# Three of the last output blocks: the residual stored first, the gated sums added onto it by DMAs with addition

## The chip, the cores and the metric

The kernel runs on one core of a Trainium2 chip. The metric is the device time of one execution in microseconds. A core has a matrix engine (PE, with its weight loads PEld), a vector engine (DVE), a scalar engine (ACT), a general one (POOL), and SP, which here only issues DMAs. ACT and POOL can issue DMAs too. All DMAs are carried out by the same 16 DMA engines. PE writes its sums to PSUM, which DVE and ACT read; POOL works on SBUF alone.

## The reference

One input x of 2048 tokens by 512 channels is normalized. Attention with 32 heads of 16 channels is computed from it, and beside it a token-mixing MLP, whose silu is the gate:

```python
x = A_x
xn = _layernorm(x, axis=-1)
s = _A_ref(xn, A_wqkv, A_wo)                            # softmax attention, times wo
g = _silu(_B_ref(xn, B_w1, B_b1, B_w2, B_b2))           # mixer over tokens: w1, gelu, w2
return x + s * g
```

Everything is float32. Matrix products in which precision counts are made of three products of upper and lower halves.

## The kernel before

The 2048 tokens are 16 blocks of 128 rows (`NB = 16`, `P = 128`, `D = 512`), so a block of the output is a tile of 128 x 512 float32, 256 KB. The kernel computes the projections, then runs one long loop in which PE alternates between the scores of attention, their row maxima, the values (`values`, whose accumulator is the bank `av`) and pieces of the mixer's and the output projection's products, which fill the gaps. The order is written out by hand; each engine executes its own instructions in that order and waits on semaphores for the others. SP's queue is in order as well.

For the output projection the four groups of heads are multiplied with wo. Of the blocks 8 to 15, three groups are summed early, the gate g of each block is loaded into a tile `gates[b]`, and `ys[b]` holds the residual x plus s times g over those three groups. The `ys` of the blocks 8 to 11 are quarters of one tile named `big`, those of 12 to 15 quarters of another. The tiles of `gates[b]` are called `wh`, `wl` or `raw` in the profile: 8 `wh`, 9 `wl`, 10 `wh`, 11 `wl`, 12 `wh`, and 13, 14 and 15 `raw`.

The last group of heads is complete only after the last step of attention. The code at the end of the kernel then does for each block 8 to 15: three matmuls (`Last.times`, L1389) of that group into a PSUM bank (`mx` or `sc`); the gate, a product of the bank with `gates[b]`, on DVE (`gate`, L1398) or, for block 10, by way of ACT and POOL (`gate_aside`, L1394 and L1395); and `send` (L1402 and L1403), an addition of `ys[b]` on POOL or DVE and a store of the result from SP's or ACT's queue. POOL adds for the blocks 8 to 12, DVE for 13 to 15. For the blocks 10 to 15 a piece of attention's own division is in between (`ways`, with the two subtractions on L107).

Of the kernel before, what the change touches and what calls it, by code (L numbers as in the profile page):

```python
# [11 lines left out]
OP = mybir.AluOpType  # L12
# [9 lines left out]
def tile_attention_token_mixer(ctx, tc, x, wqkv, wo, w1, b1, w2, b2, out):  # L22
    nc = tc.nc
    P = 128
# [78 lines left out]
    def av_bank():  # L103
        return ps_av.tile([P, 512], F32, name="av")
# [594 lines left out]
    def silu(j, ps):  # L699
        y = el.tile([P, D], F32, name="ev")  # L700
        t = el.tile([P, D], F32, name="t", bufs=4)
        nc.scalar.activation(y, ps, AF.Identity, bias=b2h[:, j : j + 1], scale=0.25)
        after(2, lambda: nc.scalar.activation(t, y, AF.Tanh))

        def gate():
            nc.gpsimd.tensor_scalar(t, t, 1.0, None, op0=OP.add)
            nc.gpsimd.tensor_tensor(out=t, in0=t, in1=y, op=OP.mult)
            after(2, lambda: nc.sync.dma_start(g_d[j], t))

        after(4, gate)  # L710
# [4 lines left out]
    def put_away(p, span, half, av):  # L715

        if (p, half) == (NP - 1, 1):
            return
        ev = el.tile([P, 512], F32, name="ev")
        copied(ev, av)  # L720
        if p == NP - 1:
            own(span, half, ev)
            return
        g, i = divmod(p, 4)
        if i == 0:
            dens[span] = sm.tile([P, 64], F32, name="d")
        rows = ev.rearrange("(j r) q -> r j q", r=32)
        for a in range(2):
            h = 2 * i + a
            nc.sync.dma_start(  # L730
                dens[span][DH * h : DH * (h + 1), :],
                rows[16 - 16 * a, 2 * a : 2 * a + 2, :].rearrange("c (j q) -> c j q", q=64),
            )
        nc.sync.dma_start(num_d[g][span][160 * i : 160 * i + P, :], ev)
        if i == 3 or p == NP - 2:
            invert(g, span)
# [165 lines left out]
    ys = {}  # L902
# [68 lines left out]
    gates = {}  # L971
# [11 lines left out]
    def step(t):  # L983

        p, r = divmod(t, SPP)
        span, i = divmod(r, NB)
        at = span * 1024
        if (p, span) != (NP - 1, QH - 1):
            return p, span, None, (i, i), (at, at + 512), i == 0, i == NB - 1
        half, i = divmod(i, NB // 2)  # L990
        at += 512 * half
        return p, span, half, (2 * i, 2 * i + 1), (at, at), i == 0, i == NB // 2 - 1
# [14 lines left out]
    def values(t):  # L1007
        p, span, half, kbs, qat, first, last = step(t)
        if first:
            state["av"] = av_bank()  # L1010
        av = state["av"]
        for a in range(2):
            for c in range(2):
                j = 2 * a + c
                nc.tensor.matmul(  # L1015
                    av[32 * j : 32 * j + 32, :],
                    vps[p][:, kbs[c], 16 * a : 16 * a + 32], prob.pop((t, a, c)),
                    start=first, stop=last,
                )
        if last:  # L1020
            soon.append(lambda: put_away(p, span, half, av))
# [357 lines left out]
    class Last:  # L1379
# [15 lines left out]
            nc.gpsimd.tensor_tensor(out=gates[self.b], in0=t, in1=gates[self.b], op=OP.mult)  # L1395

        def gate(self):
            nc.vector.tensor_tensor(out=gates[self.b], in0=self.ps, in1=gates[self.b], op=OP.mult)  # L1398

        def send(self, eng, queue=nc.sync):  # L1400
            b = self.b
# [1 line left out]
            queue.dma_start(out[b * P : (b + 1) * P, :], gates[b])  # L1403

    lasts = {}
    for b in (8, 9):
        lasts[b] = Last(b).times(3)
        lasts[b].gate()
    for v in (NT - 2, NT - 1):
        values(v)  # L1410
    for b in (8, 9):
        lasts[b].send(nc.gpsimd)
    while later or soon:
# [21 lines left out]
    ways[1].back(1, *parts_[1])  # L1435
    ways[1].upper(1, *parts_[1])
    lasts[11].gate()
    lasts[11].send(nc.gpsimd)
    ways[1].lower(1, *parts_[1])
    for b in range(12, NB):  # L1440
        lasts[b] = Last(b).times(3)
    for b in range(12, NB):
        lasts[b].gate()
    lasts[12].send(nc.gpsimd)
    lasts[13].send(nc.vector, nc.scalar)
    lasts[14].send(nc.vector)
    lasts[15].send(nc.vector, nc.scalar)

# [26 lines left out]
```

## Time and profile before

| | us |
|---|---|
| median of 3 runs | 1634.22 (1633.86 to 1634.64) |
| the profiled execution | 1634.06 |
| its span | 1632.2 |
| PE busy | 1621.9 (99%) |
| DVE busy | 1418.1 (87%) |
| ACT busy | 1194.5 (73%) |
| POOL busy | 575.4 (35%) |

The span is the time from the first to the last instruction that the profiler saw. The granted clock of PE was 0.998 of full speed over the span. In a row of the timeline the first number is the start in us, the second the duration of the group, followed by the engine, the source line, the operation, the tile that is written and those that are read, the shape, and the count. In a table by windows each engine's busy time stands in us with the number of instructions, then PE's clock, the DMA engines' busy share and their rate. In an account of one line, the numbers after a group are the least, median and largest duration of one instruction in ns, then the first and last start in us.

### The profile page before, as it was taken

Reading aid. Unit: us, or ns where it says so; the run is one execution under the profiler, and the core shown is the slowest. Engines: PE = TensorE matmul, PEld = TensorE weight load, DVE = VectorE, ACT = ScalarE, POOL = GpSimd, SP = SyncE. Lnnn points to the kernel's source line nnn. Section 1 sums busy time; section 2 is a strip of 40 time slices with the busy share of each in tenths; the row PEclk is TensorE's granted clock in tenths of the full one; section 3 lists DMA queues with packets and bytes.
Section 4 is the critical chain, followed back from the end, with each engine's and each line's share of the span. In section 5 each row is a group of like instructions: output and inputs, shape, how many; then the busy total and the mean of one; then the engine's idle time right before and its main releaser. Section 6 shows DMA issues by size and latency. Waiting matters only on the chain.

```text
span 1632.2 us, 31813 instructions
## 1 busy us (share of the span) xinstructions
PE 1621.9 (99%) x11948; PEld 892.0 (55%) x11948; DVE 1418.1 (87%) x2506; ACT 1194.5 (73%) x2297; POOL 575.4 (35%) x676
## 2 busy tenths in 40 slices
PE   9999999999999999999999999999999999999998
PEld 7888845555554545555555545555554545544554
DVE  7655989999999999999999999999999999999955
ACT  4333488777877777787777777787777777788785
POOL 0223743333443334332433223223222332662434
PEclk9999999999999999999999999999999999999999
DMA  6479621415133141836150522305152515354344
GB/s 226 174 247 227 122 59 47 82 34 95 41 53 76 38 79 35 191 121 111 37 85 18 99 57 46 70 30 77 37 85 59 91 37 78 100 110 134 117 151 168
DMA packets 150775, 152.89 MB, mean 94 GB/s; under 512 B 51340, under 2 KB 109708, under 8 KB 147548
## 3 DMA queue, kind: packets, MB, share of 16 engines
q1 hardware_dynamic: 146044, 149.70, 38.8%
q8 instruction: 94, 1.54, 0.4%
q0 software_dynamic: 4288, 0.62, 0.3%
q14 instruction: 61, 0.50, 0.1%
q10 hardware_dynamic: 288, 0.52, 0.1%
HBM read 99.63 MB, written 50.32 MB: 92 GB/s over the span
## 4 chain that ended last, share of the span: by engine, by line
PE 98%; DVE 1%; ACT 0%; DMA 0%; SPq 0%; issue 0%; DVEq 0%; ACTq 0%
PE av L1015 31%; PE sc L1165 16%; PE sc L1000 10%; PE sc L537 8%; PE mx L1000 8%; PE mx L1165 7%; PE mx L537 6%; PE sc L440 3%; PE mx L440 2%; PE mx L1112 1%; PE sc L1112 1%; PE sc L1215 1%; PE av L440 1%; PE sc L116 1%; PE sc L114 1%; PE sc L115 1%
## 5 line engine op out<-in xcount | busy, mean ns | idle before, releaser
L541 DVE TENSOR_REDUCE mxp<-sc 128x1 f32<-128x512 f32 x1129 | 735.9, 681 | 74.7 <-PE sc L537 49.7
L1005 ACT ACTIVATE prob<-sc 128x512 f32<-128x512 f32 x1135 | 638.3, 604 | 168.8 <-PE sc L1000 98.2
L541 DVE TENSOR_REDUCE mxp<-mx 128x1 f32<-128x512 f32 x919 | 606.0, 681 | 50.3 <-PE mx L537 30.9
L1005 ACT ACTIVATE prob<-mx 128x512 f32<-128x512 f32 x913 | 523.1, 606 | 127.3 <-PE mx L1000 71.7
L1015 PE MATMUL av<-prob,vp 128*32 128x512 f32 x4096 | 543.0, 604 | 0.0
L537 PE MATMUL sc<-big 48*128 48x512 f32 x1129 | 427.8, 417 | 0.0
L1000 PE MATMUL sc<-big 50*128 50x512 f32 x1135 | 423.1, 417 | 0.2 <-ACT prob L1005 0.2
L1165 PE MATMUL sc<-hu,wh 64*128 64x512 f32 x1072 | 359.3, 404 | 0.0
L537 PE MATMUL mx<-big 48*128 48x512 f32 x919 | 349.9, 416 | 0.1
L1000 PE MATMUL mx<-big 50*128 50x512 f32 x913 | 346.9, 415 | 0.5 <-ACT prob L1005 0.5
L1000 PEld LDWEIGHTS sc<-big 50*128 50x128 f32 x1135 | 198.2, 185 | 137.9 <-DVE mxp L541 102.0
L537 PEld LDWEIGHTS sc<-big 48*128 48x128 f32 x1129 | 196.9, 185 | 81.7 <-ACT prob L1005 53.5
L1165 PEld LDWEIGHTS sc<-hu,wh 64*128 64x128 f32 x1072 | 193.9, 184 | 58.8 <-issue 41.9
L1000 PEld LDWEIGHTS mx<-big 50*128 50x128 f32 x913 | 162.2, 185 | 107.4 <-DVE mxp L541 83.3
L1165 PE MATMUL sc<-hu,wl 64*128 64x512 f32 x536 | 215.1, 401 | 0.0
L537 PEld LDWEIGHTS mx<-big 48*128 48x128 f32 x919 | 160.9, 185 | 74.4 <-ACT prob L1005 38.1
L1015 PEld LDWEIGHTS av<-prob,vp 128*32 128x32 f32 x4096 | 81.8, 108 | 171.8 <-issue 161.4
L1165 PE MATMUL mx<-hu,wh 64*128 64x512 f32 x464 | 156.2, 405 | 0.0
L179 POOL CAST wh<-raw 128x512 fp32r<-128x512 f32 (+1 forms) x105 | 61.3, 584 | 255.2 <-PE sc L537 57.7
L107 POOL TENSOR_TENSOR wl<-raw,wh 128x512 fp32r<-128x512 f32 (+1 forms) x113 | 136.6, 1210 | 28.9 <-ACT wh L181 20.4
L562 POOL CAST m<-f 16x128 fp32r<-16x128 f32 x32 | 9.0, 280 | 311.2 <-DVE f L552 308.4
L1165 PEld LDWEIGHTS sc<-hu,wl 64*128 64x128 f32 x536 | 98.8, 184 | 13.3 <-issue 5.9
(240 smaller groups left out, 1592.0 us busy)
## 6 DMA issues: line engine op xcount, KB each, us to landing
raw<-in_B_w_dram SPq DMA_DIRECT2D x93, 256.0 KB
big<-k_d SPq DMA_DIRECT2D x96, 128.0 KB
big<-q_d SPq DMA_DIRECT2D x96, 128.0 KB
q_d<-sg SPq DMA_DIRECT2D x16, 512.0 KB
k_d<-sg SPq DMA_DIRECT2D x16, 512.0 KB
num_d<-ev SPq DMA_DIRECT2D x30, 256.0 KB
u_d<-uo SPq DMA_DIRECT2D x14, 512.0 KB
hu<-u_d SPq DMA_DIRECT2D x14, 512.0 KB
```

The costliest lines, as they stand in the source:

```text
L107: eng.tensor_tensor(out=o, in0=a, in1=b.bitcast(F32), op=OP.subtract)
L114: nc.tensor.matmul(ps, wh, mh, start=first, stop=False)
L115: nc.tensor.matmul(ps, wh, ml, start=False, stop=False)
L179: nc.gpsimd.tensor_copy(whs[n][:, :m, :], raws[n][:, :m, :])
L440: nc.tensor.matmul(ps, w[part][:, kd, m], xt[kd][:, z, :], start=w is wh and z == 0 and kd == 0, stop=w is wl and kd == ND - 1,)
L537: nc.tensor.matmul(ps, q[o : o + 48, r * P : (r + 1) * P], k[o : o + 48, c * 512 : (c + 1) * 512], start=True, stop=True,)
L541: return nc.vector.tensor_reduce(mxp[u // 16][:, a, r % 8, c : c + 1], ps, axis=AX.X, op=OP.max)
L1000: nc.tensor.matmul(ps, ks[p][o : o + 50, kb * P : (kb + 1) * P], qs[p][o : o + 50, at : at + 512], start=True, stop=True,)
L1005: return nc.scalar.activation(e, ps, AF.Exp, scale=scale)
L1015: nc.tensor.matmul(av[32 * j : 32 * j + 32, :], vps[p][:, kbs[c], 16 * a : 16 * a + 32], prob.pop((t, a, c)), start=first, stop=last,)
L1112: nc.tensor.matmul(ps(a), w(r), m(r), start=first, stop=last)
L1165: i = nc.tensor.matmul(ps(), w(r), m(r), start=first and first_half, stop=last and not first_half)
```

## The change

For the blocks 11, 12 and 13 the addition of the residual leaves POOL and DVE. Before the last blocks are finished, SP stores `ys[b]`, which then holds all but the last group's part, to the output. The gate of these blocks writes its product into `ys[b]` itself, in place of `gates[b]`. At the end POOL issues three DMAs that add `ys[b]` onto the rows already in the output. The blocks 14 and 15 are added on DVE and stored as before.

```diff
         def gate(self):
-            nc.vector.tensor_tensor(out=gates[self.b], in0=self.ps, in1=gates[self.b], op=OP.mult)
+            to = ys[self.b] if self.b in onto else gates[self.b]
+            nc.vector.tensor_tensor(out=to, in0=self.ps, in1=gates[self.b], op=OP.mult)
...
     lasts = {}
+    onto = ()
     for b in (8, 9):
         lasts[b] = Last(b).times(3)
         lasts[b].gate()
     for v in (NT - 2, NT - 1):
         values(v)
+    onto = (11, 12, 13)
+    for b in onto:
+        nc.sync.dma_start(out[b * P : (b + 1) * P, :], ys[b])
     for b in (8, 9):
         lasts[b].send(nc.gpsimd)
...
     lasts[11].gate()
-    lasts[11].send(nc.gpsimd)
     ways[1].lower(1, *parts_[1])
     for b in range(12, NB):
         lasts[b] = Last(b).times(3)
     for b in range(12, NB):
         lasts[b].gate()
-    lasts[12].send(nc.gpsimd)
-    lasts[13].send(nc.vector, nc.scalar)
+    for b in onto:
+        nc.gpsimd.dma_start(out[b * P : (b + 1) * P, :], ys[b], accum_op=OP.add)
     lasts[14].send(nc.vector)
     lasts[15].send(nc.vector, nc.scalar)
```

On SP, at the end of the program, the queue changes as follows; names in brackets are the semaphores waited for (DMAHW and DMASW those of DMAs issued by SP or ACT and by POOL, the others those of engines):

```order
-L1403 DMA out_dram<-wh 128x512 [waits DMAHW7_49,Pool_49]
-L1403 DMA out_dram<-wl 128x512 [waits DMAHW0_49,Pool_49]
-L1403 DMA out_dram<-wh 128x512 [waits DMAHW1_49,Pool_49]
-L1403 DMA out_dram<-wl 128x512 [waits DMAHW2_49,Pool_49]
-L1403 DMA out_dram<-wh 128x512 [waits DMAHW3_49,Pool_49]
-L1403 DMA out_dram<-raw 128x512 [waits DMAHW5_49,DVE_49]
+L1415 DMA out_dram<-big 128x512 [waits DMAHW7_49]
+L1415 DMA out_dram<-big 128x512 [waits DMAHW0_49]
+L1415 DMA out_dram<-big 128x512 [waits DMAHW1_49]
+L1404 DMA out_dram<-wh 128x512 [waits DMAHW2_49,Pool_49]
+L1404 DMA out_dram<-wl 128x512 [waits DMAHW3_49,Pool_49]
+L1404 DMA out_dram<-wh 128x512 [waits DMAHW4_49,Pool_49]
```

Three stores from `big` stand ahead of the stores of the blocks 8, 9 and 10; the stores of 11 and 12 are gone, and that of 14 follows unchanged.

On POOL, the end of the program, from the additions of the blocks 8 and 9 on:

```order
-L1402 TENSOR_TENSOR wh<-big,wh 128x512 [waits DVE_49]
-L1402 TENSOR_TENSOR wl<-big,wl 128x512 [waits DVE_49]
+L1403 TENSOR_TENSOR wh<-big,wh 128x512 [waits DVE_49]
+L1403 TENSOR_TENSOR wl<-big,wl 128x512 [waits DVE_49]
 L1395 TENSOR_TENSOR wh<-t,wh 128x512 [waits DMAHW4_49,Activation_49]
-L1402 TENSOR_TENSOR wh<-big,wh 128x512 [waits Pool_49]
-L1402 TENSOR_TENSOR wl<-big,wl 128x512 [waits DVE_49]
-L1402 TENSOR_TENSOR wh<-big,wh 128x512 [waits DVE_49]
+L1403 TENSOR_TENSOR wh<-big,wh 128x512 [waits Pool_49]
+L1449 DMA out_dram<-big 128x512 [waits DMAHW7_49,DVE_49]
+L1449 DMA out_dram<-big 128x512 [waits DMAHW0_49,DVE_49]
+L1449 DMA out_dram<-big 128x512 [waits DMAHW1_49,DVE_49]
```

The additions of the blocks 11 and 12 have given way to three DMAs, each of which waits for its residual's store (DMAHW7, 0 and 1) and its gate on DVE.

On DVE, the gates of the blocks 11 to 15 and the additions behind them:

```order
-L1398 TENSOR_TENSOR wl<-sc,wl 128x512 [waits DMAHW3_49,PE_49]
+L1399 TENSOR_TENSOR big<-sc,wl 128x512 [waits DMASW5_49,DMASW4_49,DMASW6_49,DMASW3_49,DMASW7_49,DMASW2_49,DMAHW3_49,DMASW1_49,DMAHW7_49,DMASW0_49,PE_49]
 L107 TENSOR_TENSOR hu<-mx,hu 32x256 [waits Activation_49]
-L1398 TENSOR_TENSOR wh<-mx,wh 128x512 [waits DMAHW2_49,PE_49]
-L1398 TENSOR_TENSOR raw<-mx,raw 128x512 [waits PE_49]
-L1398 TENSOR_TENSOR raw<-sc,raw 128x512 [waits PE_49] x2
-L1402 TENSOR_TENSOR raw<-big,raw 128x512 [waits DVE_49] x3
+L1399 TENSOR_TENSOR big<-mx,wh 128x512 [waits DMAHW2_49,DMAHW0_49,PE_49]
+L1399 TENSOR_TENSOR big<-mx,raw 128x512 [waits DMAHW1_49,PE_49]
+L1399 TENSOR_TENSOR raw<-sc,raw 128x512 [waits PE_49] x2
+L1403 TENSOR_TENSOR raw<-big,raw 128x512 [waits DVE_49] x2
```

One of three additions is gone from DVE, and the gates of 11, 12 and 13 wait for the stores of the residual whose tiles they overwrite. ACT's queue keeps one store of two, that of block 15.

## The prediction

> **What bounds the kernel now.** I read the page first, then the last 17 us of the timeline engine by engine, then the table by windows of the same stretch, then the accounts of single source lines.
>
> ```profile
> span 1632.2 us, 31813 instructions
> PE 1621.9 (99%) x11948; PEld 892.0 (55%) x11948; DVE 1418.1 (87%) x2506; ACT 1194.5 (73%) x2297; POOL 575.4 (35%) x676
> PE 98%; DVE 1%; ACT 0%; DMA 0%; SPq 0%; issue 0%; DVEq 0%; ACTq 0%
> ```
>
> PE holds 98% of the chain, and the change gives PE nothing to do or to leave out. So it can act only where the chain is not on PE: after the last matmul, about 1624.9 us, when seven microseconds of the span are left. They belong to DVE, then to the DMA engines. Here are DVE's rows of the end, the last store on ACT's queue, and SP's stores:
>
> ```profile
> 1621.84 0.43 DVE L107 TENSOR_TENSOR hu<-sc,hu 32x256 fp32r<-32x256 f32 x1 [0.32 <-ACT hu L771]
> 1622.30 0.69 DVE L1398 TENSOR_TENSOR wl<-sc,wl 128x512 f32<-128x512 f32 x1
> 1623.02 0.43 DVE L107 TENSOR_TENSOR hu<-mx,hu 32x256 fp32r<-32x256 f32 x1
> 1623.48 0.69 DVE L1398 TENSOR_TENSOR wh<-mx,wh 128x512 f32<-128x512 f32 x1
> 1624.09 0.68 DVE L1398 TENSOR_TENSOR raw<-mx,raw 128x512 f32<-128x512 f32 x1
> 1624.69 1.28 DVE L1398 TENSOR_TENSOR raw<-sc,raw 128x512 f32<-128x512 f32 x2
> 1625.88 2.49 DVE L1402 TENSOR_TENSOR raw<-big,raw 128x512 f32<-128x512 f32 x3
> 1628.40 0.34 ACTq L1403 DMA_DIRECT2D out_dram<-raw  x1
> ```
> ```profile
> 1606.11 9.97 SPq L966 DMA_DIRECT2D out_dram<-t  x4
> 1618.41 0.33 SPq L1403 DMA_DIRECT2D out_dram<-wh  x1
> 1619.63 0.33 SPq L1403 DMA_DIRECT2D out_dram<-wl  x1
> 1624.18 0.33 SPq L1403 DMA_DIRECT2D out_dram<-wh  x1
> 1625.42 0.33 SPq L1403 DMA_DIRECT2D out_dram<-wl  x1
> 1626.64 0.33 SPq L1403 DMA_DIRECT2D out_dram<-wh  x1
> 1627.80 0.33 SPq L1403 DMA_DIRECT2D out_dram<-raw  x1
> ```
>
> L1398 at 1622.30 is the gate of block 11, then come those of 12, 13, 14 and 15; the three L1402 are the additions of 13, 14 and 15. DVE has no gap from 1621.84 to 1625.88 + 2.49 = 1628.37, and the store of block 15 is issued 0.03 us later, at 1628.40. SP's stores are, from 1618.41 on, blocks 8, 9, 10, 11, 12 and 14. What comes after the last issue is in the windows and in the account of the closing line:
>
> ```profile
> core 0: us, PE busy (x) PEld busy (x) DVE busy (x) ACT busy (x) POOL busy (x), PEclk, DMA share, GB/s
> 1618.00:1619.00 1.00, 0.84 (x8) 0.00 (x0) 0.00 (x0) 0.09 (x1) 1.00 (x2) 1.00 0.00 0
> 1619.00:1620.00 1.00, 0.67 (x5) 0.59 (x6) 0.19 (x1) 0.56 (x2) 0.60 (x1) 1.00 0.70 262
> ...
> 1628.00:1629.00 1.00, 0.00 (x0) 0.00 (x0) 0.37 (x1) 0.00 (x0) 0.00 (x0) 0.50 1.03 383
> 1629.00:1630.00 1.00, 0.00 (x0) 0.00 (x0) 0.00 (x0) 0.00 (x0) 0.00 (x0) 0.50 1.03 381
> 1630.00:1631.00 1.00, 0.00 (x0) 0.00 (x0) 0.00 (x0) 0.00 (x0) 0.00 (x0) 0.50 0.27 98
> 1631.00:1632.00 1.00, 0.00 (x0) 0.00 (x0) 0.00 (x0) 0.00 (x0) 0.00 (x0) 0.50 0.00 0
> ```
> ```profile
> L1471 SPq DRAIN  x3: 7/7/13, 1631.4 to 1631.7; - x3
> ```
>
> From 1628 to 1630 the 16 DMA engines are full at 383 GB/s, so one block of 256 KB (262,144 bytes) takes 0.68 us of them. Stores were issued every 0.6 us from 1626.64 on, faster than that, so the last one queues. SP's first drain, at 1631.4, says that all stores have landed: 3.0 us after the issue of block 15. The closing handshake takes 0.8 us more to 1632.2, and 1.86 us lie outside the span (1634.06 us for this execution, against a median of 1634.22). **The end is thus set by two things in a row: when DVE releases the last store, and when the DMA queue has emptied.** The change shortens the first and lengthens the second.
>
> **What it removes.** POOL's rows of the end, and the account of line L1402:
>
> ```profile
> 1622.86 1.29 POOL L1402 TENSOR_TENSOR wh<-big,wh 128x512 f32<-128x512 f32 x1
> 1624.11 1.29 POOL L1402 TENSOR_TENSOR wl<-big,wl 128x512 f32<-128x512 f32 x1
> 1625.35 1.27 POOL L1402 TENSOR_TENSOR wh<-big,wh 128x512 f32<-128x512 f32 x1
> ...
> L1402 DVE TENSOR_TENSOR raw<-big,raw x3: 678/679/1284, 1625.9 to 1627.7; 128x512 f32<-128x512 f32 x3
> ```
>
> POOL loses the additions of blocks 11 and 12, 1.29 + 1.27 us, on no path of their own. DVE loses that of block 13. It is the slow one of the three, 1.28 us against 0.68, and the only one that runs while POOL adds too (until 1626.62). Without it the additions of 14 and 15 start at 1625.88 and follow at 0.60 us: the last ends at 1625.88 + 0.60 + 0.68 = 1627.16, and block 15 is issued at about 1627.2, **1.2 us earlier**. If they should still be slowed by what POOL then does, each would take 1.28 and the issue would be at 1628.4, as now; that is the lower end of this gain, zero. I take 1.2, since the two additions that now run without a POOL addition take 0.68.
>
> **What it adds on SP.** Three stores of the residual, queued behind the last L966, whose row ends at 1606.11 + 9.97 = 1616.08, and ahead of block 8's store at 1618.41. SP is free there for 2.33 us. Three issues of 0.33 us, or 0.5 with the spacing that crowded issues could have, are 1.0 to 1.5 us: hidden. Were they not, the stores of 8 and 9 would be later, and SP has nothing after them until 1624.18. Their bytes (3 x 0.68 = 2.0 us) move around 1617 to 1619, where the window 1618 to 1619 shows idle DMA engines. The first to need them is DVE's gate of block 11 at 1622.30, which overwrites the residual's tile. With the 3.0 us of the slowest store, block 11's residual has landed by about 1619.1, and block 13's by 1620.2 against a gate at 1624.09. So three microseconds are to spare, and the cost is zero; if the cover were gone, DVE would stand still with all gates behind it and every microsecond would show at the end.
>
> **What it adds on DVE.** The gate of block 11 is listed with ten DMA semaphores instead of one, eight of them of POOL's DMAs into the same tile's memory.
>
> ```profile
> L1398 DVEq EVENT_SEMAPHORE  x3: 21/21/21, 1616.3 to 1622.6; - x3
> L111 POOL DMA_DIRECT2D big<-m x128: 497/517/596, 190.0 to 1572.8; - x128
> ```
>
> Those DMAs were issued by 1572.8, 50 us before, so nothing is waited for. The waits themselves are instructions of 0.021 us; five of them (two semaphores each) run in the sequencer beside the preceding subtraction of 0.43 us. Between zero and, if none were hidden, 0.1 us: I take zero.
>
> **What it adds on POOL and the DMA engines.** This is the unknown: no DMA with addition is in the trace. For the issue, the neighbours are POOL's two kinds of plain DMA, with their landing (from issue to landed) as given in the accounts of their tiles, m first, ones second:
>
> ```profile
> DMA to landing us min/median/max: 1.5/1.6/4.5
> ...
> L126 POOL DMA_DIRECT2D big<-ones x4: 798/828/1048, 125.4 to 142.8; - x4
> DMA to landing us min/median/max: 3.9/6.5/8.8
> ```
>
> An issue costs 0.50 (4 KB from 8 partitions) to 1.05 us (16 KB from 128 partitions). The new tile has 128 partitions, so I take the median of the second, 0.83. POOL is free after block 10's addition, 1622.86 + 1.29, about 1624.1; block 11's gate is done by 1622.99, 12's by 1624.17 and 13's by 1624.77, so POOL waits for none and issues at 1624.1, 1624.9 and 1625.8, until 1626.6. Nothing is queued behind these on POOL but the closing handshake.
>
> The first bytes: m's DMA lands 1.6 us after its issue begins, 0.5 of it issue, with next to no bytes; of the other 1.1 I put half ahead of the bytes and half behind. So bytes of block 11 move from 1624.1 + 0.83 + 0.5, about 1625.4.
>
> How long they move: an addition must at least write what a store writes, 0.68 us. At most, by the nearest rows, a block takes as much as the worst landing of a DMA of POOL, 8.8 us. It has to read the old rows of the output and write the new ones, so I take a load followed by a store, 2 x 0.68 = 1.37 us per block, near the lower end, because these rows are long like a store's, whereas those of ones moved in 128-partition scraps beside other traffic.
>
> The sum of DMA work from 1625.4: what remains of block 10's store, about 0.4 (issued at 1624.18; block 8's, issued at 1618.41, moved only after 1619.0, by the windows); three additions, 4.1; blocks 14 and 15, 1.4. That is 5.9 us, so the bytes end at 1631.3. Block 15, released at 1627.2, is not last any more, or shares the engines with the additions. Half a microsecond for landing gives 1631.8 where 1631.4 stood: +0.4 us, **1634.06 + 0.4, about 1634.5 us**. The 1.2 us that DVE saves are used up by 2.0 us of additional DMA work.
>
> The Trainium skill has a price for such additions: its page "Collectives: The Full Stack", in the section "The bandwidth ceiling: the fold count and why AG ≠ RS ≠ AR", holds that a reducing DMA loses half of the rate because it reads two sources per write, 62.28 against 32.35 GB/s as measured there. By that ratio of 1.93 an addition would be an estimated 1.32 us here and the time 1634.4; no run so far shows it.
>
> **The rivals.**
>
> *Additions as cheap as stores.* If the second read overlaps fully, an addition costs 0.68. The work ends well before, and the last event is block 15, issued 1.2 us earlier into a shorter queue: 1.2 to 1.9 us less, about 1632.5. For it: the DMA engines' share in the windows is for packets with one read and one write, and reading could be free. Against it: at 383 GB/s these engines are full with one of each.
>
> *Additions are slow: slower than before.* If each row is read, added and written before the next goes on, a block could cost four stores, 2.7 us. From 1625.4 the work is 0.4 + 8.2 + 1.4 = 10.0 us, landed at 1635.9, +4.5: 1638.6. For it: POOL's own DMAs of merely 16 KB took up to 8.8 us to land; the third addition, issued at 1625.8, would land at 1634.6 even at that price without its own bytes. Against it: m's typical 1.6 us. It makes the kernel slower by over 0.2% (3.3 us, about what a measurement can tell from no change) from the point where landing passes 1631.4 + 3.3, that is, from 2.35 us per block.
>
> *DVE and POOL still in each other's way.* The additions of 14 and 15 take 1.28 each, as 13's did beside POOL; block 15 is issued at 1628.4 as now, behind the additions' bytes: about 1634.7. For it: the one slow row. Against it: POOL then issues DMAs and adds nothing. The Trainium skill, "SBUF — State Buffer", section "Who interferes with whom", has a DVE instruction with two SBUF inputs contend only with a GpSimd instruction that reads SBUF. The 1284 against 679 ns agree with its first half; no row here shows the second.
>
> **How the numbers follow.** Forecast 0.54; cheap additions 0.23; slow ones by over 0.2% 0.19; the conflict 0.03; anything faster by over 0.2% 0.01, since even an immediate landing after DVE's end could hardly save 3.3 us. So faster 0.01, within 0.2% 0.80, slower 0.19. The range goes from the cheap case, 1632.3, to 1638.0, an addition at about 2.5 us.
>
> **What would show it.** On DVE two L1403 additions of about 0.68 us each, ending near 1627.2; gates that start where they do now; three POOL issues of 0.5 to 1.05 us from 1624.1; at the end SP waiting for the DMAs of POOL, not for block 15, with DMA engines busy until about 1631. The forecast is wrong if SP's first drain moves below 1630.5 (additions cheap) or beyond 1633, if the gate of block 11 stands after 1622.5, or if rows before 1616 move at all.

## The result and the profile after

| | us | runs |
|---|---|---|
| before, median | 1633.82 (1632.83 to 1635.15) | 19 |
| changed, median | 1636.31 (1635.51 to 1637.73) | 19 |
| ratio | 1.0017, 95% interval 1.0011 to 1.0023 | |
| profiled execution, changed | 1637.12, span 1635.3 | 1 |

The changed kernel is 2.5 us slower by the medians, 0.15 to 0.17%: clear of the noise, but below the 0.2% that the prediction called a change. It lies within the range of 1632.3 to 1638.0, 1.8 us above the predicted 1634.5. Here and below, ratios and intervals leave out three stray executions (4806 to 8348 us), which the medians of their kernels still count.

The timeline of the changed kernel from block 11 on; first DVE, then the last store on ACT's queue, then POOL:

```profile
1622.09 0.43 DVE L107 TENSOR_TENSOR hu<-sc,hu 32x256 fp32r<-32x256 f32 x1 [0.32 <-ACT hu L771]
1622.59 0.69 DVE L1399 TENSOR_TENSOR big<-sc,wl 128x512 f32<-128x512 f32 x1
1623.31 0.43 DVE L107 TENSOR_TENSOR hu<-mx,hu 32x256 fp32r<-32x256 f32 x1
1623.77 0.69 DVE L1399 TENSOR_TENSOR big<-mx,wh 128x512 f32<-128x512 f32 x1
1624.38 0.68 DVE L1399 TENSOR_TENSOR big<-mx,raw 128x512 f32<-128x512 f32 x1
1624.98 1.28 DVE L1399 TENSOR_TENSOR raw<-sc,raw 128x512 f32<-128x512 f32 x2
1626.18 1.28 DVE L1403 TENSOR_TENSOR raw<-big,raw 128x512 f32<-128x512 f32 x2
...
1627.49 0.37 ACTq L1404 DMA_DIRECT2D out_dram<-raw  x1
...
1624.34 2.75 POOL L1449 DMA_DIRECT2D out_dram<-big  x3
```

Block 11's gate begins at 1622.59 where it began at 1622.30. The whole end is shifted that far already ahead of the edit (block 8's gate, too, starts 0.26 us later), and in the ten other kernels below block 11's gate starts anywhere from 1621.28 to 1622.87. Its start is therefore taken as zero in what follows. DVE did what was forecast: two additions, 1.28 us together, the last one ending at 1627.46, and block 15's store issued 4.90 us behind the gate instead of 6.10. The end nevertheless comes 12.7 us behind it instead of 9.9. The DMA engines' windows and the accounts of POOL's DMAs and of the closing line say where that went:

```profile
1625.00:1626.00 1.00, 0.12 (x1) 0.00 (x0) 1.00 (x3) 0.00 (x0) 1.00 (x3) 1.00 0.73 260
1626.00:1627.00 1.00, 0.00 (x0) 0.00 (x0) 1.00 (x3) 0.00 (x0) 1.00 (x2) 1.00 0.98 104
1627.00:1628.00 1.00, 0.00 (x0) 0.00 (x0) 0.46 (x1) 0.00 (x0) 0.09 (x1) 1.00 1.11 176
1628.00:1629.00 1.00, 0.00 (x0) 0.00 (x0) 0.00 (x0) 0.00 (x0) 0.00 (x0) 1.00 0.99 123
1629.00:1630.00 1.00, 0.00 (x0) 0.00 (x0) 0.00 (x0) 0.00 (x0) 0.00 (x0) 1.00 1.08 223
1630.00:1631.00 1.00, 0.00 (x0) 0.00 (x0) 0.00 (x0) 0.00 (x0) 0.00 (x0) 0.59 1.09 266
1631.00:1632.00 1.00, 0.00 (x0) 0.00 (x0) 0.00 (x0) 0.00 (x0) 0.00 (x0) 0.50 1.07 330
1632.00:1633.00 1.00, 0.00 (x0) 0.00 (x0) 0.00 (x0) 0.00 (x0) 0.00 (x0) 0.50 0.40 90
```
```profile
L1449 POOL DMA_DIRECT2D out_dram<-big x3: 957/1193/1517, 1624.3 to 1625.6; - x3
...
DMA to landing us min/median/max: 4.2/7.0/7.9
...
L1475 SPq EVENT_SEMAPHORE  x12: 17/28/28, 1633.5 to 1635.3; - x12
...
L1475 POOLq DRAIN  x3: 46/112/8752, 1625.3 to 1635.1; - x3
L1475 SPq DRAIN  x3: 7/7/13, 1634.5 to 1634.8; - x3
```

The share is as full as in the kernel before, near 1.0 for six microseconds, but it carries 104 to 176 GB/s in the first three of them and 223 to 330 in the others, against 383. The third addition is issued at 1625.58 (the last start, 1625.6) and lands 7.9 us later, at 1633.5. Only then does SP's first closing check (the semaphore instruction at 1633.5) go through; its first drain follows at 1634.5, a whole microsecond later, and the span ends at 1635.3.

### The profile page after: what moved, and what is told of

Its sections match the earlier page's. It is cut to its first block, busy times and chain, and to the rows that moved or that the text cites. A ratio compares the mean times of both kernels' runs of the same rounds, so it can differ in the third digit from the quotient of the medians.

```text
span 1635.3 us, 31818 instructions
## 1 busy us (share of the span) xinstructions
PE 1621.9 (99%) x11948; PEld 887.8 (54%) x11948; DVE 1416.7 (87%) x2505; ACT 1194.4 (73%) x2297; POOL 578.0 (35%) x677
## 4 chain that ended last, share of the span: by engine, by line
PE 96%; DVE 2%; ACT 1%; POOL 0%; DMA 0%; issue 0%; SPq 0%; DVEq 0%; POOLq 0%
PE av L1015 31%; PE sc L1165 16%; PE sc L1000 10%; PE sc L537 8%; PE mx L1000 8%; PE mx L1165 7%; PE mx L537 7%; PE sc L440 2%; PE mx L440 2%; PE mx L1112 1%; PE sc L1112 1%; PE sc L1215 1%; PE av L440 0%; PE sc L354 0%; DMA xr<-in_A_x_dram 0%; PE sc L116 0%
```

## The experiments

Three questions: what an addition costs, whether POOL's queue or the addition itself costs it, and why a release on DVE that is 1.2 us earlier bought nothing. All kernels, each with its own profiled execution; the columns in the middle are in us behind the start of block 11's gate, from the timeline and the account of the closing line. DMA work is the engines' share in the window from 1624 us to 1636 times its 12 us, which is the time that the packets took, per engine; that window moves the same 132 GB/s, six blocks, in all but the two kernels marked.

| kernel | median, us | before beside it | ratio (95%) | block 15 issued | SP's first drain | end | DMA work |
|---|---|---|---|---|---|---|---|
| before | | | | 6.1 | 9.1 | 9.9 | 4.3 |
| changed | 1636.31 | 1633.82 | 1.0017 (1.0011 to 1.0023) | 4.9 | 11.9 | 12.7 | 7.4 |
| drop_adds | 1632.02 | 1633.61 | 0.9993 (0.9984 to 1.0002) | 4.9 | 7.7 | 8.5 | 2.2 (66 GB/s) |
| plain_stores | 1631.94 | 1633.61 | 0.9991 (0.9982 to 1.0000) | 4.9 | 7.6 | 8.4 | 4.3 |
| one_11 | 1633.60 | 1633.34 | 1.0001 (0.9991 to 1.0010) | 5.8 | 9.2 | 10.0 | 5.5 |
| one_12 | 1634.06 | 1633.34 | 1.0005 (0.9996 to 1.0014) | 5.5 | 9.5 | 10.3 | 5.4 |
| four | 1636.58 | 1633.34 | 1.0017 (1.0008 to 1.0026) | 4.4 | 12.3 | 13.1 | 8.3 |
| shift2 | 1636.61 | 1633.61 | 1.0017 (1.0009 to 1.0026) | 4.9 | 11.1 | 12.3 | 7.3 |
| pool_last | 1633.87 | 1633.54 | 1.0003 (0.9994 to 1.0012) | 6.4 | 9.6 | 10.4 | 4.2 (131 GB/s) |
| psum_add | 1633.57 | 1633.34 | 1.0000 (0.9991 to 1.0009) | 5.5 | 9.2 | 10.0 | 4.3 |
| stores_only | 1634.30 | 1633.61 | 1.0005 (0.9996 to 1.0014) | 6.1 | 9.5 | 10.3 | 4.3 |
| interleaved | 1632.86 | 1633.54 | 0.9996 (0.9988 to 1.0005) | 5.5 | 8.6 | 9.5 | 4.3 |

### Without the additions

```diff
-    for b in onto:
-        nc.gpsimd.dma_start(out[b * P : (b + 1) * P, :], ys[b], accum_op=OP.add)
```

> The changed kernel without its three DMAs with addition; the blocks 11, 12 and 13 keep the residual and the first three groups of heads but lack the last group's part. If the saving on DVE is real and only the additions eat it, block 15's store is issued at about 1627.2 us as in the changed kernel, follows two plain stores and lands about 1.8 us earlier than before: 1632.0 us, ratio to before about 0.999, with SP's first closing drain near 1629.5. If instead the early stores or the longer list of waits on the gates cost time, it stays at 1633.8 or above.

Measured 1632.02 us, 1.6 less than before beside it, though the interval just holds no change; SP's first drain came at 1629.4, and the end is 8.5 us behind the gate instead of 9.9. The rest of the change, then, costs nothing large; the three DMAs make the loss. Since three blocks fewer are stored at the end, this run does not show what the rest would be worth.

### The same DMAs without addition

```diff
-        nc.gpsimd.dma_start(out[b * P : (b + 1) * P, :], ys[b], accum_op=OP.add)
+        nc.gpsimd.dma_start(out[b * P : (b + 1) * P, :], ys[b])
```

> The changed kernel with POOL's three DMAs issued without addition, so that they overwrite the residual: the output of the blocks 11, 12 and 13 lacks it. Same queue, same bytes written, no second read. If the price is the addition itself (178 ns a row of 2 KB where a store takes 86), the DMA work behind 1626 shrinks by about 3 us and POOL's DMAs land within 3 to 5 us of their issue: 1633.0 to 1634.0 us. If the price is POOL's queue, whatever it carries, landing stays at 7 to 8 us and the time at 1636.

Measured 1631.94 us, better than the first theory's 1633.0, with an interval that reaches exactly to no change; the end is 1.5 us nearer to the gate than before, with as many bytes. The window of the whole end and the account of POOL's DMAs, of the changed kernel first and of this one second:

```profile
1624.00:1636.00 12.00, 1.12 (x5) 0.58 (x4) 3.46 (x6) 0.00 (x0) 3.09 (x4) 0.76 0.62 132
```
```profile
1624.00:1636.00 12.00, 0.24 (x2) 0.00 (x0) 2.59 (x5) 0.00 (x0) 1.22 (x3) 0.80 0.36 132
...
1625.00:1626.00 1.00, 0.00 (x0) 0.00 (x0) 1.00 (x3) 0.00 (x0) 0.22 (x1) 1.00 1.07 373
...
L1449 POOL DMA_DIRECT2D out_dram<-big x3: 539/555/652, 1623.5 to 1624.7; - x3
...
DMA to landing us min/median/max: 2.9/3.0/3.1
```

The same bytes are written (132 GB/s in both), on the same queue and in the same order. With addition the DMA engines need 0.62 x 12 = 7.4 us, without 0.36 x 12 = 4.3: an addition takes 1.04 us more than a store. A store is 0.72 by drop_adds (three in 2.2 us), so an addition is 1.76 us, 2.4 stores. Landing falls from between 4.2 and 7.9 us to between 2.9 and 3.1, and an issue on POOL from 1.0 to 1.5 us to 0.54 to 0.65. The rival, POOL's queue as such, falls. The plain DMAs also move in fewer packets (80 for a block, see the last section, against 144), but that is not the reason: a plain store from SP has 144 as well, and the 0.72 us are those of stores from SP and ACT.

The packets in the traces say more about the 1.76 us. The median row of 2 KB takes 178 ns in an addition of the changed kernel and 86 in a store of the kernel before, about two stores. But 70 of the 384 rows take more than 190 ns, up to 1.03 us, and the mean is 215. What holds these rows up is open; a lone addition has such rows too (32 of 128 in one_11).

### One addition, and four

one_11 and one_12 leave one block with the new form, four adds block 14 to the three. The edit of one_12:

```diff
-    onto = (11, 12, 13)
+    onto = (12,)
...
     lasts[11].gate()
+    lasts[11].send(nc.gpsimd)
...
+    lasts[13].send(nc.vector, nc.scalar)
```

> Only block 12 by a DMA with addition: POOL adds block 11 and then issues one addition at about 1625.4 us, DVE adds 13, 14 and 15. If an addition costs about 1.7 us of the DMA engines and shares them with what is queued, this lone one lands 3.5 to 4.5 us after its issue, near 1629.7, ahead of block 15's store. DVE's addition of 13 meets no POOL addition any more (0.68 instead of 1.28 us), so block 15 is issued at 1627.8 instead of 1628.4, and the engines have 1.0 us more to move: 1633.3 to 1634.5 us. If a DMA with addition has a fixed landing of 7 to 8 us, it lands at 1633 and the time is 1635.5 or more.

> Only block 11 by a DMA with addition, issued by POOL at about 1624.1 us, ahead of POOL's addition of 12, which still runs beside DVE's addition of 13. With a price of 1.7 us on the engines it lands near 1628.3, its work lies in the pauses of the DMA engines before 1627, and the end is that of before within 0.5 us: 1633.5 to 1634.3 us. With a fixed landing of 7 to 8 us it lands near 1632, behind block 15's store, and the time is 1634.5 or more.

> Block 14 as well by a DMA with addition, four in all. Per block the engines have 1.7 us in place of the 0.7 us of a store, so the last landing is about 1.0 us later than in the changed kernel: 1637.3 us. If landing were set by a fixed latency from the issue, the fourth issue, some 0.6 us behind the third, would make it 1636.9; if by DVE, whose chain is 0.6 us shorter again, 1635.7.

One_12 came out as the theory of a price on the engines has it: landing 4.3 us behind the issue, DVE's three additions in 1.88 us, and a time 0.7 us above before, within the noise. In one_11 the addition landed after 4.1 us, and the time was 1633.60 us. A fixed landing of 7 to 8 us falls with both: it takes that long only behind other additions. Four took 1636.58, less than the 1637.3 expected, and its interval (1634.6 to 1637.6 us) holds all three theories; in the profile the end is 0.4 us later than with three, where 1.0 was expected. Its work on the engines, 8.3 us, does fit, at 1.7 us per addition once 1.5 for two stores is taken off. The three sizes, one, three and four, give 1.7 to 1.9 us each. The end in the table moves with them, but not by their work alone, since a first one fits into pauses of the engines: it comes 10.0 and 10.3 us behind the gate with one, 12.7 with three and 13.1 with four.

### What comes behind the last landing

In the closing, SP checks one semaphore after the other in a fixed order, and in the changed kernel the first check is the one that waits for the third addition: it goes through at 1633.5, and the others follow until the first drain at 1634.5. Two small DMAs issued long before move the additions on by two semaphores:

```diff
         if s == NU:
+            for _ in range(2):
+                nc.gpsimd.dma_start(spare_d, ones)
```

> The changed kernel with two small DMAs of 16 KB from POOL into an unused tensor, issued some 60 us before the end, so that the semaphores of the three additions move on by two. SP's closing checks then wait for the last addition sixth instead of first. If the checks behind the one that lands last cost about 1 us, the interval from the last landing to SP's first closing drain shrinks from 1.0 to about 0.4 us and the time by about 0.5 us, to 1635.8. If the order of the checks is without effect, the interval stays at 1.0 and the time at 1636.3.

The accounts of its additions and of its closing line:

```profile
L1452 POOL DMA_DIRECT2D out_dram<-big x3: 942/1212/1529, 1624.6 to 1625.8; - x3
...
DMA to landing us min/median/max: 4.1/6.1/7.9
...
L1478 POOLq DRAIN  x3: 46/108/8792, 1625.6 to 1634.9; - x3
L1478 SPq DRAIN  x3: 7/7/13, 1634.0 to 1634.7; - x3
```

The third addition lands at 1625.8 + 7.9 = 1633.7 and SP's first drain follows at 1634.0: 0.3 us instead of 1.0. The interval went as the first theory expected, the time did not: 1636.61. The end comes at 1635.2, still 1.5 us behind the landing against 1.8, because POOL's own drain, which began at 1625.6 and lasted 8.79, ends only at 1634.4, and the end of the span comes 0.8 us behind that. So the order of the checks is worth 0.7 us at SP and 0.3 at the end, too little to see in the medians.

The other side of it, the kernel before with a plain DMA of POOL's at the end:

```diff
-    lasts[15].send(nc.vector, nc.scalar)
+    lasts[15].send(nc.vector, nc.gpsimd)
```

> The kernel before with one edit: block 15's store, the last, is issued by POOL and not by ACT, without addition. If a DMA of POOL's that lands last costs the closing 0.7 to 0.9 us (SP checks its semaphore ahead of the others, and POOL's drain ends only 0.6 us behind the landing), the time from the last landing to the end is 1.6 to 1.8 us instead of 0.9 and the kernel takes 1634.3 to 1635.0 us. If the closing costs the same whoever issued, it stays within 0.3 us of 1633.5.

```profile
L1403 POOL DMA_DIRECT2D out_dram<-raw x1: 654/654/654, 1627.7 to 1627.7; - x1
...
DMA to landing us min/median/max: 2.4/2.4/2.4
...
L1471 SPq DRAIN  x3: 7/7/13, 1630.9 to 1631.2; - x3
```

Landed at 1627.65 + 2.4 = 1630.05, ended at 1631.7: 1.65 us, as expected for a DMA of POOL's that lands last. The time, 1633.87, is 0.3 above before and not told apart from it, and lies in neither theory's range. In the profile the end is 0.5 us later: the closing is 0.7 us longer than before (there the last store lands at 1631.27, 1.0 us before the end), and POOL issues 0.29 us behind DVE's end where ACT did after 0.03, but the store landed after 2.4 us instead of 2.9.

### DVE's saving by itself

```diff
-    lasts[13].send(nc.vector, nc.scalar)
+    held_ps = any_bank()
+    nc.scalar.copy(held_ps, ys[13])
+    nc.vector.tensor_tensor(out=gates[13], in0=held_ps, in1=gates[13], op=OP.add)
+    nc.scalar.dma_start(out[13 * P : 14 * P, :], gates[13])
```

> The kernel before, all stores plain, with one edit: ACT, idle since 1622.5, copies the residual of block 13 into a PSUM bank, and DVE adds it from there, so that this addition reads one operand of SBUF instead of two. If the 1.28 us of this addition in the kernel before came from POOL's addition beside it, it takes about 0.7 us here and block 15's store is issued 0.6 us earlier: 1633.2 us, against 1633.7. If its length has another cause, it stays at 1.28 and the time at 1633.7.

```profile
L1447 DVE TENSOR_TENSOR raw<-sc,raw x1: 677/677/677, 1625.1 to 1625.1; 128x512 f32<-128x512 f32 x1
...
1626.00:1627.00 1.00, 0.00 (x0) 0.00 (x0) 0.97 (x2) 0.00 (x0) 0.00 (x0) 1.00 0.47 174
1627.00:1628.00 1.00, 0.00 (x0) 0.00 (x0) 0.00 (x0) 0.00 (x0) 0.00 (x0) 0.90 1.04 385
1628.00:1629.00 1.00, 0.00 (x0) 0.00 (x0) 0.00 (x0) 0.00 (x0) 0.00 (x0) 0.50 1.04 383
1629.00:1630.00 1.00, 0.00 (x0) 0.00 (x0) 0.00 (x0) 0.00 (x0) 0.00 (x0) 0.50 0.47 170
```

POOL's addition runs beside it until 1625.8, yet with one operand in PSUM DVE's takes 0.68 us instead of 1.28; and in one_12, where POOL adds nothing at that time, the same addition takes 0.68 us with both operands in SBUF (three in 1.88 us). Together the two settle the reason for the slow addition. This is what the Trainium skill, "SBUF — State Buffer", section "Who interferes with whom", leads one to expect. DVE seems to stand still rather than to run slowly: in the kernel before, stores_only, pool_last and one_11 the slow addition ends 0.55 to 0.56 us behind POOL's, whether it takes 1.28 us or, as in one_11, 0.98. But the time, 1633.57 against 1633.34, shows no gain (an interval of 1.5 us either way would hide one of 0.6), and the end lies 10.0 us behind the gate as against 9.9, although block 15's store is issued 0.6 us earlier. The engines are full through 1627 and 1628 and empty at about the same distance from the gate as before: the four stores from block 12 on wait for one another, and the last one only waits longer. So the earlier issue alone bought nothing in this profile. In drop_adds and plain_stores, where it came with a queue that was emptier, or filled earlier (in plain_stores the engines are full from 1625 on), it did count: there SP's first drain comes 2.8 and 2.7 us behind block 15's issue, before 3.0, and here 3.7.

### The early stores alone

The kernel before with the three stores of the residual added at the same place, and nothing else changed:

```diff
     for v in (NT - 2, NT - 1):
         values(v)
+    for b in (11, 12, 13):
+        nc.sync.dma_start(out[b * P : (b + 1) * P, :], ys[b])
```

> The kernel before with only the three early stores of the residual added; the blocks are finished and stored over them as before. If these are hidden, the time is that of before within 0.3 us (1633.8), with the same rows on DVE from block 11's gate on. If they hold up SP's later stores or take DMA time that the end needs, it is slower by 0.5 us or more.

1634.30 against 1633.61, and the interval of 0.9996 to 1.0014 holds both theories. All rows as far as the issue of block 15 stand where they did (6.1 us behind the gate), so the gates were not held up. The end is 0.4 us later, as is SP's first drain. The trace has most of it in the closing. Three more DMAs move the last stores on to other semaphores, and block 15's is now checked earlier in SP's list: its check goes through at 1631.25 us, with six more behind it, and the first drain comes 0.44 us later. In the kernel before its check, at 1631.29, has one behind it, and the drain comes after 0.13 us. So 0.3 of the 0.4 us are the order of the checks, and the stores are hidden within 0.1 us.

### Another order without additions

If the time at which the queue fills is what counts, the stores of 12 to 15 should be ready earlier and one after the other:

```diff
+    banks = {}
+    for b in (12, 14, 15):
+        banks[b] = any_bank()
+        nc.scalar.copy(banks[b], ys[b])
+
+    def send_from_bank(b, queue):
+        nc.vector.tensor_tensor(out=gates[b], in0=banks[b], in1=gates[b], op=OP.add)
+        queue.dma_start(out[b * P : (b + 1) * P, :], gates[b])
+
+    lasts[12].gate()
+    lasts[13].gate()
+    send_from_bank(12, nc.scalar)
+    lasts[13].send(nc.gpsimd)
+    lasts[14].gate()
+    lasts[15].gate()
+    send_from_bank(14, nc.sync)
+    send_from_bank(15, nc.scalar)
```

> No DMA with addition; the end of the kernel before in another order. ACT copies the residuals of 12, 14 and 15 into PSUM banks, DVE gates 12 and 13, adds 12 from its bank, gates 14 and 15, adds both from their banks; POOL adds 11 and 13. Stores become ready at about 1625.4 (11 and 12), 1626.7, 1627.2 and 1627.8 us where they were at 1625.4, 1626.6, 1627.2, 1627.8 and 1628.4. If the DMA queue's filling from block 12 on sets the end, as the earlier release of block 15 alone was worth nothing, filling it 1.2 us earlier brings the last landing about 1 us forward: 1632.6 us. If DVE's last instruction sets it, 0.6 us are gained: 1633.0. If neither, 1633.5.

Measured 1632.86 against 1633.54, the lowest median of those that compute the whole output, but the interval, 0.9988 to 1.0005, holds no change. In the profile the end is 9.5 us behind the gate, 0.4 to 0.5 less than before and than psum_add, which issues block 15 at the same 5.5 us. So far as two profiled executions can show it, having the queue filled earlier is thus worth something where the earlier last issue was worth nothing, though less than the 1 us expected.

## Why the prediction came out as it did

The direction was right (a little slower, within 0.2%), and the account of the 1.2 us on DVE against additional DMA work was the right one to draw up. The size was not right: 0.4 us was forecast, and 2.5 came by the medians, about 2.8 in the profiled executions, counted from block 11's gate. Two terms of the sum were too small, both on the same side, and the time still stayed under the 0.2% (3.3 us); that was in part luck. By one of its own signs the forecast failed: SP's first drain was not to come beyond 1633, and it came at 1634.5. (Block 11's gate stood after 1622.5 too, but with the whole end, which was late ahead of the edit already.) Point by point:

- **SP and the early stores: right, as far as the gates go.** SP issued them between its last L966 and block 8's store, and block 11's gate began 0.50 us behind the start of the subtraction ahead of it, where it had been 0.46. So the ten semaphores cost 0.04 us. In stores_only the last landing, too, stayed within 0.1 us.
- **DVE's saving: right in size, wrong in worth.** Block 15 was issued 1.2 us earlier. The prediction had the end set by DVE's release and the queue "in a row"; in psum_add's profile, behind block 12, the queue alone set it, and in the changed kernel the additions fill that queue.
- **POOL's issues: 0.83 us forecast, 0.96 to 1.52 measured**, 2.75 for three instead of 2.5. The neighbour that I chose, a plain DMA of 128 partitions, is not one for an addition; a plain store of the same tile takes 0.54 to 0.65.
- **The bytes: this is the mis-sized term.** A block was put at "a load followed by a store, 2 x 0.68 = 1.37 us"; it took 1.76 by the work on the engines, 2.4 stores. The median row, 178 ns against 86, is close to the load and store of the prediction; the slow rows were not in it. Over three blocks that is 1.2 us, and with the later issues the last landing moved from the 1631.8 forecast to 1633.5, or 1633.2 counted from the gate: 1.4 us. The Trainium skill's ratio of 1.93 ("Collectives: The Full Stack", section "The bandwidth ceiling: the fold count and why AG ≠ RS ≠ AR") would have been further off; by the runs here it is 2.4 for the whole of an addition.
- **The closing: a term that was missing.** The prediction let SP's first drain coincide with the last landing, as it could for a store that is checked late. The third addition is checked first: 1.8 us from landing to the end instead of the 0.8 counted, about 1 us (in shift2, with another order, POOL's own drain leaves 1.5). Together with the bytes, 0.4 + 1.4 + 1.0 = 2.8.

Of the rivals, cheap additions are out (plain_stores shows what they would have given, 1631.94, not the 1632.5 worked out). Additions of 2.7 us per block are out as well; the measured price lies between the forecast's 1.37 us and the 2.35 from which 0.2% would have been passed. DVE and POOL were not in each other's way: both additions took 0.68 us beside POOL's issues.

## What to carry to other kernels

Before moving an addition from an idle or half-idle engine into a DMA, see whether the DMA queue is empty at that point: at the end of this kernel, where the last stores fill it, an addition of 256 KB occupied it for 2.4 stores, and shortening the compute chain by more than a microsecond bought nothing back. Where the last stores are issued faster than the DMA engines move them (every 0.6 us against 0.68 here), what sets the end is when the queue begins to be full for good, and not the issue of the last store alone; so the first of the last stores are worth bringing forward. That much the profiles of psum_add and interleaved show, one execution each; the medians could not tell. And a DMA from POOL that landed last made the closing 0.5 to 0.9 us longer.

## What the runs showed of the hardware

- A plain DMA from POOL with 128 rows of 2 KB was cheap: 0.54 to 0.65 us of issue, and a lone one landed after 2.4 us. By the queue rows of the profile it moves in larger packets: POOL's queue has 80 more packets with one such store than the 4288 of before, but 144 more with one addition of the same tile, for the same bytes.
- The price of an addition hardly depended on company: 1.7 to 1.9 us of the DMA engines with one, three or four of them. Landing did depend on it: 4.1 to 4.3 us for a lone one, up to 7.9 for the third.
- Behind a DMA of POOL's that lands last, the closing took 1.5 to 1.8 us, in four kernels (changed, four, shift2, pool_last).
- A DVE addition with both operands in SBUF, begun beside one of POOL's, ended 0.55 to 0.56 us behind that one in four traces; with one operand in PSUM it took its usual 0.68 us.
